# Experts' second product with tokens on the partitions, and an earlier pick of the first block

## The chip, the cores and the metric

One core of one Trainium2 chip. The metric is the device time of one execution in microseconds (us). All tensors are fp32.

## What is computed

```python
num = einsum('bhsm,bhmd->bhsd', phi(q), einsum('bhsm,bhsd->bhmd', phi(k), v))   # attention with random features
x = (num / den).reshape(2304, 512)
x = maximum(0.01 * (x @ w_in), x @ w_in) @ w_out           # dense, hidden width 2048
e = argmax(x @ w_gate, axis=1)                             # one of 8 experts for each token
gate = softmax(x @ w_gate)[e] * sigmoid(x @ w_output_gate)[e]
out[mask_e] = gate * (maximum(x[mask_e] @ w1[e], 0) @ w2[e])     # 512 -> 1024 -> 512, mask_e: tokens of expert e
```

With the inputs of the case the experts that have tokens get 576, 576 and 1152 of the 2304, and of the first 1792 tokens (chunks 0 to 6 below) 576, 576 and 640 are theirs.

## The kernel before

Every fp32 factor of the large products is split into two F32R parts, hi and lo (`hi_lo`, L208 on ScalarE for hi, L211 on VectorE for lo), and a product is three matmuls: hi·hi, lo·hi, hi·lo.

**Dense stage.** Tokens go in 9 chunks (0 to 8) of 256. For a chunk `c` and a step `u` of 8, `h_unit` makes 256 columns of the hidden layer (24 matmuls of 256 moving columns, L462 to L464), ScalarE copies them (L467), VectorE applies the leaky step (L468) and makes `gh` (L210) and `gl` (L211); `x_unit` adds their part of the output (12 matmuls of 512 columns, L481 to L483). The main loop writes `h_unit` of the next pair ahead of `x_unit` of this one, so TensorE runs H(8,1), X(8,0), H(8,2), X(8,1) and so on. When a chunk is done, `route_item` transposes its rows (L506), makes the gate's logits, picks an expert for each token, scatters the tokens' numbers into the table `tab_d` (L593, two indirect DMAs issued by GpSimd) and writes the rows to `x1_d` in DRAM (L597, SyncE's queue). Routing of chunk c runs beside chunk c+1, that of chunk 8 beside the first block of the experts.

**Experts.** A slot is 576 tokens of one expert, and a block is half a slot (288 tokens). Four slots are needed here. `Slot` reads the slot's part of the table into `idx` (L658) and loads 8 weight pieces of 512 KB (`weight(k)`, L664 and L666, on SyncE's queue) through two raw buffers (`wst`, tag `wraw`, 2 buffers) and converts each (hi L208 on ScalarE, lo L211 on VectorE). A block gathers its rows (`rows`, L681, 3 indirect DMAs of 96 rows), transposes them (`xt`, L692, 3 transposes for each of 4 pieces `d`), makes 8 pieces of the hidden layer (`hidden`, 12 matmuls of 288 columns each, L705 to L707; then ScalarE's relu L708 and VectorE's rest L709), and then the output with features on the partitions (`back`, for each of 4 `d` 24 matmuls of 288 columns, L718 to L720, copied by ScalarE, L721). `store` turns this into rows of tokens (4 transposes for each of 3 groups, L729), scales them (L731, L733) and scatters them to the output (L734).

The first slot is picked by `early()` among the experts whose first 576 tokens are known to be there, when chunk 7 has been routed, that is, while chunk 8 runs; its idx, its 8 weights (two for each of the last four steps of chunk 8) and the rows of its first block come then. All other slots come from `listed()`, after chunk 8's routing. A block's rows are gathered while the block before it runs (`following.rows()` at f == 3), its transposes stand between the `back(d)` of the block before. SyncE waits for the table (`behind`) before idx.

A scheduler writes the order on each engine, and an engine takes its instructions in that order. The order that matters is that of ScalarE and VectorE, which share weight conversion, the dense stage's `g`, and what the experts' products need.

Of the kernel before, what the change touches and what calls it, by code (L numbers as in the profile page):

```python
# [14 lines left out]
I32 = mybir.dt.int32  # L15
# [19 lines left out]
HALF = SLOT // 2  # L35
SUB = 96
NSUB = HALF // SUB
# [50 lines left out]
def tile_kernel(ctx: ExitStack, tc: tile.TileContext, kT, k_nat, v_nat, qT, q_nat, om, w_in, w_out, wg, w1, w2, out, stop=None, dbg=None):  # L88
# [46 lines left out]
    with ExitStack() as pa:  # L135
# [23 lines left out]
        def pads():  # L159
            padv = wst.tile([P, NE * NBLK * SLOT // P], I32, name="padv", tag="w32")  # L160
            nc.gpsimd.iota(padv, pattern=[[0, NE * NBLK * SLOT // P]], base=NTOK, channel_multiplier=0)
            nc.sync.dma_start(tab_d.rearrange("(p n) o -> p (n o)", p=P), padv)

            zero = wst.tile([P, 2, ROW], F32, name="zero", tag="wraw")
            nc.gpsimd.memset(zero, 0.0)
            nc.sync.dma_start(x1_d[NTOK - CH:NTOK, :].rearrange("(t p) n -> p t n", p=P), zero)
            nc.sync.dma_start(x1_d[NTOK:NTOK + 1, :], zero[0:1, 0, :])
# [332 lines left out]
        def route_item(c, rows):  # L500
            st = {}

            def tr(t):
                tv = ps_h.tile([P, D], F32, name="rtp", tag="h")
                for d in range(ND):
                    nc.tensor.transpose(tv[:, d * P:(d + 1) * P], rows[:, t, d * P:(d + 1) * P], ident)  # L506
                if t == 0:
                    if eb is None:
                        th = sb.tile([P, ND, CH], F32R, name="rth", tag="xh", bufs=3)
                        tl = sb.tile([P, ND, CH], F32R, name="rtl", tag="xl", bufs=3)  # L510
                    else:
                        th = eb.tile([P, ND, CH], F32R, name="rth", tag="eyr", bufs=1)
                        tl = eb.tile([P, ND, CH], F32R, name="rtl", tag="ey", bufs=1)
# [128 lines left out]
        tabv = tab_d.rearrange("(c p i) o -> c p (i o)", p=SUB, i=2 * NSUB)  # L642
# [5 lines left out]
        class Slot:  # L648


            def __init__(self, num, exp, at, first=False):
                self.c = nc.values_load(num[0:1, ds(at, 1)], engines=[SP], min_val=0, max_val=NC - 1)
                self.e = nc.values_load(exp[0:1, ds(at, 1)], engines=[SP], min_val=0, max_val=NE - 1)
                self.first = first
                self.w = []
                pool = rt if first else eb
                self.idx = pool.tile([SUB, 2 * NSUB], I32, name="idx", tag="idx", bufs=1 if first else 3)
                got = nc.sync.dma_start(self.idx, tabv[ds(self.c, 1)].rearrange("o p i -> (o p) i"))  # L658
                behind(got.ins, [o for k, o in placed if k == placed[-1][0]], "the table whole")
# [12 lines left out]
        class Block:  # L672
            def __init__(self, slot, half):
                self.slot = slot
                self.idx = slot.idx[:, half * NSUB:(half + 1) * NSUB]
                self.first = slot.first and half == 0

            def rows(self):
                self.xr = eo.tile([SUB, NSUB, ROW], F32, name="exr", tag="exr", bufs=2)
                for i in range(NSUB):  # L680
                    nc.gpsimd.indirect_dma_start(  # L681
                        out=self.xr[:, i, :], out_offset=None, in_=x1_d[:, :],
                        in_offset=bass.IndirectOffsetOnAxis(ap=self.idx[:, i:i + 1], axis=0))

            def xt(self, d):
                if d == 0:
                    pool, bufs = (eo, 1) if eb is None else (eb, 2)
                    self.xh = pool.tile([P, ND, HALF], F32R, name="exh", tag="exh", bufs=bufs)
                    self.xl = pool.tile([P, ND, HALF], F32R, name="exl", tag="exl", bufs=bufs)
                t = ps_proj.tile([P, 512], F32, name="ext", tag="pj")[:, 0:HALF]  # L690
                for i in range(NSUB):
                    nc.tensor.transpose(t[:, i * SUB:(i + 1) * SUB], self.xr[:, i, d * P:(d + 1) * P], ident[0:SUB, 0:SUB])  # L692
                hi_lo(self.xh[:, d, :], self.xl[:, d, :], t, nc.scalar, nc.vector)
                if d == ND - 1:
                    self.scale = eo.tile([SUB, NSUB], F32, name="esc", tag="esc", bufs=3)
                    nc.gpsimd.tensor_copy(self.scale, self.xr[:, :, D])

            def hidden(self, f):
                if f == 0:
                    self.hh = eb.tile([P, EFF // P, HALF], F32R, name="ehh", tag="ehh", bufs=1)  # L700
                    self.hl = eb.tile([P, EFF // P, HALF], F32R, name="ehl", tag="ehl", bufs=1)
                t = ps_a.tile([P, 512], F32, name="eht", tag="a")[:, 0:HALF]
                for d in range(ND):
                    wh, wl = (w[:, f * P:(f + 1) * P] for w in self.slot.w[d])
                    nc.tensor.matmul(t, wh, self.xh[:, d, :], start=d == 0, stop=False)  # L705
                    nc.tensor.matmul(t, wh, self.xl[:, d, :], start=False, stop=False)  # L706
                    nc.tensor.matmul(t, wl, self.xh[:, d, :], start=False, stop=d == ND - 1)  # L707
                nc.scalar.activation(self.hh[:, f, :], t, AF.Relu)  # L708
                nc.vector.scalar_tensor_tensor(self.hl[:, f, :], t, 0.0, f32(self.hh[:, f, :]), op0=ALU.max, op1=ALU.subtract)  # L709

            def back(self, d):
                if d == 0:
                    self.y = eb.tile([P, ND, HALF], F32, name="ey", tag="ey", bufs=1)
                t = ps_x.tile([P, 512], F32, name="eyt", tag="x")[:, 0:HALF]
                nf = EFF // P
                for f in range(nf):
                    wh, wl = (w[:, (f % 2) * D + d * P:(f % 2) * D + (d + 1) * P] for w in self.slot.w[4 + f // 2])
                    nc.tensor.matmul(t, wh, self.hh[:, f, :], start=f == 0, stop=False)  # L718
                    nc.tensor.matmul(t, wh, self.hl[:, f, :], start=False, stop=False)  # L719
                    nc.tensor.matmul(t, wl, self.hh[:, f, :], start=False, stop=f == nf - 1)  # L720
                nc.scalar.copy(self.y[:, d, :], t)  # L721

            def store(self, i, apart=True, final=False):
                if i == 0:
                    self.yr = eb.tile([SUB, NSUB, D], F32, name="eyr", tag="eyr", bufs=1)
                ps, tag = (ps_a, "a") if final and i == 2 else (ps_h, "h")
                t = ps.tile([P, 512], F32, name="eot", tag=tag)[0:SUB]
                for d in range(ND):
                    nc.tensor.transpose(t[:, d * P:(d + 1) * P], self.y[:, d, i * SUB:(i + 1) * SUB], ident)  # L729
                if i == 1:  # L730
                    nc.scalar.activation(self.yr[:, i, :], t, AF.Copy, scale=self.scale[:, i:i + 1])  # L731
                else:
                    nc.vector.tensor_scalar_mul(self.yr[:, i, :], t, self.scale[:, i:i + 1])  # L733
                ins = nc.gpsimd.indirect_dma_start(  # L734
                    out=out[:, :], out_offset=bass.IndirectOffsetOnAxis(ap=self.idx[:, i:i + 1], axis=0),
                    in_=self.yr[:, i, :], in_offset=None, bounds_check=NTOK - 1, oob_is_err=False)
# [64 lines left out]
        for i, (c, u) in enumerate(pairs):  # L801
# [28 lines left out]
            if c == NCH - 1 and not flow and not routes:  # L830
                if slot is None:
                    slot = early()
                    block = Block(slot, 0)
                    pq.close()
                    eo = ctx.enter_context(tc.tile_pool(name="eo", bufs=2, side="right", reuse_waits="tile"))
                    block.rows()
                for k in range(len(slot.w), 8 if u == NU - 1 else min(8, len(slot.w) + 2)):
                    slot.weight(k)
# [24 lines left out]
    with ExitStack() as pb:  # L863
        eb = pb.enter_context(tc.tile_pool(name="eb", bufs=2, reuse_waits="tile"))
        late = [f for it in routes for f in it if f is not nop]
        prev = None
        for s in range(NSLOT + 1):
            for half in range(2):
                last = s == NSLOT and half == 1
                for f in range(EFF // P):  # L870
                    block.hidden(f)
                    if prev is not None and 1 <= f <= NSUB:
                        prev.store(f - 1)
# [11 lines left out]
                for d in range(ND):  # L885
# [5 lines left out]
        for i in range(NSUB):  # L891
            prev.store(i, final=True)

        n_slots = nc.values_load(nsl[0:1, 0:1], min_val=NSLOT, max_val=NSLOT + NE)
        with tc.For_i(NSLOT, n_slots) as s:  # L895
# [3 lines left out]
            for half in range(2):  # L899
# [6 lines left out]
                for d in range(ND):  # L906
                    b_.back(d)
                for i in range(NSUB):
                    b_.store(i, False)
# [69 lines left out]
```

## Time and profile before

| | |
|---|---|
| median of 3 runs | 900.98 us (895.33 to 901.02) |
| the profiled execution | 894.16 us, span 892.4 us |
| TensorE busy | 834.9 us, 94% of the span |
| mean granted clock of TensorE | 0.983 |
| VectorE, ScalarE, GpSimd busy | 456.5, 316.7, 184.5 us |

The profile gives each instruction's start and duration on its engine; matmuls are pipelined, so a matmul's rate is read from the distance between two starts and not from its duration. A number in brackets behind an instruction is the time that the engine stood idle before it, with what ended that. Engines: PE is TensorE, PEld its weight load, ACT ScalarE, DVE VectorE, POOL GpSimd, SP SyncE (SPq: its DMA queue). [...]

### The profile page before, as it was taken

To read this page: it belongs to the slowest core of one execution; us is meant where nothing else is said; L and a number is where in the kernel's file an instruction comes from. 1 tells how busy PE (TensorE), PEld (TensorE's weight loads), DVE (VectorE), ACT (ScalarE), POOL (GpSimd) and SP (SyncE) were. 2 spreads that over 40 slices of the span, in tenths; PEclk is the share of its full clock that TensorE was granted. 3 is DMA by queue.
4 is the path that set the end of the run, shared out by engine and by line. 5 is a ranking of instruction groups with operands and counts; after the bars stand their busy time and mean duration, and the time that the engine had idled before them with its cause. 6 is when DMAs were issued, how large, how long until landed. Compare 5 with 4: busy or idle time off the path is not lost. (4 is left out here: it accounts for less than half of the span.)

```text
span 892.4 us, 14811 instructions
## 1 busy us (share of the span) xinstructions
PE 834.9 (94%) x5699; PEld 757.9 (85%) x5699; DVE 456.5 (51%) x1149; ACT 316.7 (35%) x783; POOL 184.5 (21%) x257
## 2 busy tenths in 40 slices
PE   9789898899899999999999999998759899999995
PEld 7678776799799899888889898987759899999994
DVE  6999789535445455545454444344625433522220
ACT  4766556333333223323332232112414423422221
POOL 3645535202121011121010000001033112311111
PEclk9999999999999999999999999999979999999998
DMA  7646655101442021242020000005156532500001
GB/s 228 206 134 191 195 160 164 59 4 58 64 98 66 8 41 48 54 89 66 1 48 1 24 1 2 24 25 168 48 150 193 166 100 77 172 26 29 28 28 29
DMA packets 45564, 73.07 MB, mean 82 GB/s; under 512 B 5681, under 2 KB 28337, under 8 KB 45490
## 3 DMA queue, kind: packets, MB, share of 16 engines
q1 hardware_dynamic: 41842, 62.61, 25.0%
q0 software_dynamic: 3648, 9.47, 3.8%
q8 instruction: 47, 0.77, 0.4%
q14 instruction: 27, 0.22, 0.1%
HBM read 62.00 MB, written 10.07 MB: 81 GB/s over the span
## 5 line engine op out<-in xcount | busy, mean ns | idle before, releaser
L462 PE MATMUL hp<-xh,wih 128*128 128x256 f32 x576 | 166.4, 289 | 2.7 <-DVE xl L211 2.1
L463 PE MATMUL hp<-xl,wih 128*128 128x256 f32 x576 | 161.9, 281 | 0.1
L464 PE MATMUL hp<-xh,wil 128*128 128x256 f32 x576 | 161.5, 280 | 0.0
L481 PE MATMUL acc<-woh,gh 128*128 128x512 f32 x288 | 123.1, 428 | 7.0 <-DVE gh L210 5.6
L318 ACT ACTIVATE h<-pw,bias 128x128 f32<-128x128 f32 x288 | 84.8, 373 | 105.1 <-DVE bias L310 85.4
L468 DVE SCALAR_TENSOR_TENSOR g<-hp,g 128x512 f32<-128x512 f32 x72 | 49.6, 688 | 133.3 <-ACT g L467 121.9
L483 PE MATMUL acc<-woh,gl 128*128 128x512 f32 x288 | 115.0, 400 | 0.2 <-DVE gl L211 0.2
L482 PE MATMUL acc<-wol,gh 128*128 128x512 f32 x288 | 114.1, 396 | 0.0
L462 PEld LDWEIGHTS hp<-xh,wih 128*128 128x128 f32 x576 | 108.8, 189 | 6.2 <-issue 2.5
L463 PEld LDWEIGHTS hp<-xl,wih 128*128 128x128 f32 x576 | 108.8, 189 | 2.2 <-DVE xl L211 0.3
L464 PEld LDWEIGHTS hp<-xh,wil 128*128 128x128 f32 x576 | 108.8, 189 | 0.0
L467 ACT COPY g<-hp 128x512 f32<-128x512 f32 x72 | 42.3, 587 | 131.9 <-PE hp L464 131.7
L705 PE MATMUL eht<-exh,ewh 128*128 128x288 f32 x256 | 80.0, 313 | 2.4 <-ACT exh L208 1.4
L706 PE MATMUL eht<-exl,ewh 128*128 128x288 f32 x256 | 77.2, 302 | 1.3 <-DVE exl L211 1.3
L718 PE MATMUL eyt<-ehh,ewh 128*128 128x288 f32 x256 | 78.2, 305 | 0.0
L719 PE MATMUL eyt<-ehl,ewh 128*128 128x288 f32 x256 | 76.8, 300 | 0.3 <-DVE ehl L709 0.3
L707 PE MATMUL eht<-exh,ewl 128*128 128x288 f32 x256 | 76.8, 300 | 0.0
L720 PE MATMUL eyt<-ehh,ewl 128*128 128x288 f32 x256 | 76.5, 299 | 0.0
L289 PE MATMUL pw<-om_raw,xpair 128*128 128x256 f32 (+1 forms) x260 | 70.3, 385 | 3.3 <-ACT h L318 3.3
L269 POOL TENSOR_TENSOR nat<-nat 128x256 f32<-128x256 f32 (+1 forms) x65 | 44.7, 690 | 139.0 <-DMA nat<-q_nat 65.8
L481 PEld LDWEIGHTS acc<-woh,gh 128*128 128x128 f32 x288 | 54.2, 188 | 18.8 <-DVE gh L210 6.5
L483 PEld LDWEIGHTS acc<-woh,gl 128*128 128x128 f32 x288 | 54.0, 188 | 14.3 <-DVE gl L211 2.4
(157 smaller groups left out, 1552.8 us busy)
## 6 DMA issues: line engine op xcount, KB each, us to landing
eraw<-w SPq DMA_DIRECT2D x32, 512.0 KB
wraw<-w_in SPq DMA_DIRECT2D x16, 512.0 KB
wraw<-w_out SPq DMA_DIRECT2D x16, 512.0 KB
x_d<-rows SPq DMA_DIRECT2D x9, 514.0 KB
xpair<-qT SPq DMA_DIRECT2D x18, 256.0 KB
nat<-q_nat SPq DMA_DIRECT2D x30, 128.0 KB
nat<-k_nat SPq DMA_DIRECT2D x27, 128.0 KB
xpair<-kT SPq DMA_DIRECT2D x12, 256.0 KB
```

Source lines behind the costliest of these rows:

```text
L318: nc.scalar.activation(h[:, j, :], src[:, j // 2, j % 2], AF.Exp, bias=bias[:, j:j + 1], scale=sc)
L462: nc.tensor.matmul(hp[:, i, :], a, xh[:, d, :], start=d == 0, stop=False)
L463: nc.tensor.matmul(hp[:, i, :], a, xl[:, d, :], start=False, stop=False)
L464: nc.tensor.matmul(hp[:, i, :], b_, xh[:, d, :], start=False, stop=d == ND - 1)
L481: nc.tensor.matmul(acc[t], a, h_, start=u == 0 and i == 0, stop=False)
L482: nc.tensor.matmul(acc[t], a, l_, start=False, stop=False)
L483: nc.tensor.matmul(acc[t], b_, h_, start=False, stop=u == NU - 1 and i == 1)
L705: nc.tensor.matmul(t, wh, self.xh[:, d, :], start=d == 0, stop=False)
L706: nc.tensor.matmul(t, wh, self.xl[:, d, :], start=False, stop=False)
L707: nc.tensor.matmul(t, wl, self.xh[:, d, :], start=False, stop=d == ND - 1)
L718: nc.tensor.matmul(t, wh, self.hh[:, f, :], start=f == 0, stop=False)
L719: nc.tensor.matmul(t, wh, self.hl[:, f, :], start=False, stop=False)
```

## The change

`back` works on a tile of up to 128 tokens: the hidden tile is stationary and 512 columns of the weight move, so the output has tokens on the partitions and is scaled and scattered straight away. `store`, its transposes and the copy `ey` are gone. A slot's 576 tokens are 5 tiles (four of 128 and one of 64), and the blocks are 256 and 320 tokens. The first slot is picked when chunk 6 has been routed (`early()` at c == NCH - 2); the rows of both its blocks are gathered at the start of chunk 8, and its 8 weights are loaded one for each step of chunk 8.

```diff
+PARTS = [[(0, P), (1, P)], [(2, P), (3, P), (4, SLOT - 4 * P)]]
...
             def rows(self):
-                self.xr = eo.tile([SUB, NSUB, ROW], F32, name="exr", tag="exr", bufs=2)
-                for i in range(NSUB):
+                self.xr = eo.tile([P, 3, ROW], F32, name="exr", tag="exr", bufs=2)
+                for j, (i, r) in enumerate(self.tiles):
                     nc.gpsimd.indirect_dma_start(
-                        out=self.xr[:, i, :], out_offset=None, in_=x1_d[:, :],
...
-            def back(self, d):
...
+            def back(self, j, apart=True, final=False):
+                i, r = self.tiles[j]
...
+                t = ps_x.tile([P, D], F32, name="eyt", tag="x")[0:r]
                 nf = EFF // P
                 for f in range(nf):
...
+                    wh, wl = (w[:, (f % 2) * D:(f % 2 + 1) * D] for w in self.slot.w[4 + f // 2])
+                    a, b_ = (h[:, f, j * P:j * P + r] for h in (self.hh, self.hl))
+                    nc.tensor.matmul(t, a, wh, start=f == 0, stop=False)
+                    nc.tensor.matmul(t, a, wl, start=False, stop=False)
+                    nc.tensor.matmul(t, b_, wh, start=False, stop=f == nf - 1)
+                scale = self.scale[0:r, j:j + 1]
+                if final and j == 2:
+                    nc.scalar.activation(yr[:, 0:D // 2], t[:, 0:D // 2], AF.Copy, scale=scale)
+                    nc.vector.tensor_scalar_mul(yr[:, D // 2:D], t[:, D // 2:D], scale)
+                elif j == 1:
+                    nc.vector.tensor_scalar_mul(yr, t, scale)
                 else:
...
+                    nc.scalar.activation(yr, t, AF.Copy, scale=scale)
...
+            if c == NCH - 1 and u == 0:
+
+                assert not flow and slot is not None
+                pq.close()
+                eo = ctx.enter_context(tc.tile_pool(name="eo", bufs=2, side="right", reuse_waits="tile"))
+                block, second = Block(slot, 0), Block(slot, 1)
+                block.rows()
+                second.rows()
...
-            if c == NCH - 1 and not flow and not routes:
-                if slot is None:
-                    slot = early()
...
-                for k in range(len(slot.w), 8 if u == NU - 1 else min(8, len(slot.w) + 2)):
-                    slot.weight(k)
+            if slot is None and c == NCH - 2 and not routes and not any(c_ < 0 for c_, _ in flow):
+                slot = early()
+            if c == NCH - 1:
+                slot.weight(u)
...
-                        following = Block(slot, 1) if half == 0 else Block(other, 0)
-                        following.rows()
-                for d in range(ND):
-                    block.back(d)
-                    if not last:
-                        following.xt(d)
-                prev, block = block, None if last else following
+                        following = second if s == half == 0 else Block(slot, 1) if half == 0 else Block(other, 0)
+                        if following is not second:
+                            following.rows()
+                for j in range(len(block.tiles)):
+                    if not last and j < 2:
+                        following.xt(2 * j)
+                        following.xt(2 * j + 1)
+                    block.back(j, final=last)
+                block = None if last else following
```

What is not shown: idx is read by two DMAs instead of one, `x1_d`'s rows of the chunks not yet routed are filled with zeros, and two small buffers change their tags.

On GpSimd, before, from the table's scatters of chunks 6 to 8 on (L593); `exr` are a block's gathered rows, `esc` its scales:

```order
L593 DMA tab_d<-tokid,r_pi 18432x1 x4
L681 DMA exr<-x_d,idx 96x514 x3
L696 COPY esc<-exr 96x3
L593 DMA tab_d<-tokid,r_pi 18432x1 x2
L681 DMA exr<-x_d,idx 96x514 x6
```

and now, from the scatters of chunk 6 on:

```order
L594 DMA tab_d<-tokid,r_pi 18432x1 x2
L685 DMA exr<-x_d,idx 128x514 x4
L685 DMA exr<-x_d,idx 64x514
L700 COPY esc<-exr 128x2 x2
L703 COPY esc<-exr 64x1
L594 DMA tab_d<-tokid,r_pi 18432x1 x4
```

The gathers of both blocks of the first slot now stand ahead of the table's scatters of chunks 7 and 8; before, the first block's stood behind those of chunk 7 and the second block's behind those of chunk 8.

On ScalarE in chunk 8, before; `ewh` is the hi part of a weight piece of the first slot, `g` the dense stage's copy:

```order
L208 CAST ewh<-eraw 128x1024 x2
L467 COPY g<-hp 128x512
L208 CAST ewh<-eraw 128x1024 x2
L467 COPY g<-hp 128x512
L208 CAST ewh<-eraw 128x1024 x2
L467 COPY g<-hp 128x512
L208 CAST ewh<-eraw 128x1024 x2
```

and now, from the first weight piece on:

```order
L209 CAST ewh<-eraw 128x1024
L468 COPY g<-hp 128x512
L860 COPY rows<-acc_6125 128x512
L209 CAST ewh<-eraw 128x1024
L468 COPY g<-hp 128x512
L209 CAST rth<-rtp 128x4x128
L209 CAST ewh<-eraw 128x1024
L209 CAST rth<-rtp 128x4x128
L209 CAST exh<-ext 128x256
L529 COPY side<-lgp 32x256
L209 CAST ewh<-eraw 128x1024
L468 COPY g<-hp 128x512
```

Weight pieces stood in pairs ahead of the copies `g` of the last steps; now they stand one by one, spread over the chunk.

On VectorE where the first slot's first block ends and its second begins, now; `exl` is the lo part of the second block's transposed rows, `ewl` that of the second slot's weights, `ehl` that of the hidden layer:

```order
L717 SCALAR_TENSOR_TENSOR ehl<-eht,ehh 128x256 x2
L212 TENSOR_TENSOR exl<-ext,exh 128x320 x2
L212 TENSOR_TENSOR ewl<-eraw,ewh 128x1024 x2
L212 TENSOR_TENSOR exl<-ext,exh 128x320 x2
L212 TENSOR_TENSOR ewl<-eraw,ewh 128x1024
L738 TENSOR_SCALAR eyr<-eyt,esc 128x512
L212 TENSOR_TENSOR ewl<-eraw,ewh 128x1024
L717 SCALAR_TENSOR_TENSOR ehl<-eht,ehh 128x320
L212 TENSOR_TENSOR ewl<-eraw,ewh 128x1024
L717 SCALAR_TENSOR_TENSOR ehl<-eht,ehh 128x320 x2
```

Two weight pieces of the second slot stand ahead of the last two pieces of the second block's rows, and four stand ahead of the rest of its first hidden piece; ScalarE's order is the same in kind.

## Rows read from the trace of the kernel before

**Rows 1.** The page's parts 1 and 2: busy time, and PE in 40 slices.

```profile
PE 834.9 (94%) x5699; PEld 757.9 (85%) x5699; DVE 456.5 (51%) x1149; ACT 316.7 (35%) x783; POOL 184.5 (21%) x257
...
PE   9789898899899999999999999998759899999995
```

**Rows 2.** Windows: stretch, busy time (x instructions) of each engine, PEclk granted clock, DMA.

```profile
584.94:634.19 49.25, 41.48 (x259) 34.90 (x257) 25.31 (x57) 14.30 (x23) 4.92 (x6) 0.99 0.35 109
...
710.00:720.00 10.00, 8.50 (x52) 8.20 (x53) 5.84 (x8) 4.86 (x10) 4.49 (x4) 0.83 0.58 161
```

**Rows 3.** Waits of PE from 610 us on: total us, times, longest.

```profile
PE ext L692 <- DMA exr<-x_d,idx: 10.0, 3, 6.6
PE acc L481 <- DVE gh L210: 5.6, 3, 2.6
```

**Rows 4.** Timeline of PE at the second block's transposes: start, duration, instruction, [idle before].

```profile
653.78 0.29 PE L720 MATMUL eyt<-ehh,ewl 128*128 128x288 f32 x1
660.66 0.42 PE L692 MATMUL ext<-ident,exr 96*128 96x96 f32 x1 [6.58 <-DMA exr<-x_d,idx]
...
664.95 0.42 PE L692 MATMUL ext<-ident,exr 96*128 96x96 f32 x1 [3.12 <-DMA exr<-x_d,idx]
...
665.71 0.44 PE L720 MATMUL eyt<-ehh,ewl 128*128 128x288 f32 x1
...
670.75 0.34 PE L720 MATMUL eyt<-ehh,ewl 128*128 128x288 f32 x1
```

**Rows 5.** Timeline of PE: matmuls of 512, then of 288 columns, a half-slot's period, the end.

```profile
622.49 0.39 PE L481 MATMUL acc<-woh,gh 128*128 128x512 f32 x1
...
624.36 0.40 PE L483 MATMUL acc<-woh,gl 128*128 128x512 f32 x1
...
876.00 0.29 PE L718 MATMUL eyt<-ehh,ewh 128*128 128x288 f32 x1
...
879.97 1.62 PE L729 MATMUL eot<-ident,ey 128*96 128x128 f32 x12
...
802.56 0.49 PE L729 MATMUL eot<-ident,ey 128*96 128x128 f32 x3
...
830.47 0.60 PE L729 MATMUL eot<-ident,ey 128*96 128x128 f32 x4
```

**Rows 6.** Timeline of PE in chunk 8: the stalls of its last steps.

```profile
627.82 0.50 PE L481 MATMUL acc<-woh,gh 128*128 128x512 f32 x1 [2.56 <-DVE gh L210]
...
633.26 1.22 PE L692 MATMUL ext<-ident,exr 96*128 96x96 f32 x6 [2.12 <-DVE exl L211]
634.19 0.59 PE L705 MATMUL eht<-exh,ewh 128*128 128x288 f32 x1
```

**Rows 7.** Timelines of ACT and DVE: weight pieces converted.

```profile
622.01 1.05 ACT L208 CAST ewh<-eraw 128x1024 fp32r<-128x1024 f32 x1 [2.47 <-DMA eraw<-w]
...
628.19 1.05 ACT L208 CAST ewh<-eraw 128x1024 fp32r<-128x1024 f32 x1 [2.27 <-DMA eraw<-w]
...
662.70 1.04 ACT L208 CAST ewh<-eraw 128x1024 fp32r<-128x1024 f32 x1 [11.35 <-DMA eraw<-w]
...
625.47 1.22 DVE L211 TENSOR_TENSOR ewl<-eraw,ewh 128x1024 fp32r<-128x1024 f32 x1 [1.16 <-ACT ewh L208]
```

**Rows 8.** Timelines of POOL and of SP's queue: scatters, gathers, first weight of slot 1.

```profile
560.38 0.97 POOL L593 DMA_INDIRECT tab_d<-tokid,r_pi  x1 [0.30 <-issue]
...
607.55 0.96 POOL L681 DMA_INDIRECT exr<-x_d,idx  x1 [9.93 <-DMA idx<-tab_d]
...
613.65 0.18 POOL L696 COPY esc<-exr 96x3 f32<-96x3 f32 x1 [2.69 <-DMA exr<-x_d,idx]
...
648.11 0.96 POOL L593 DMA_INDIRECT tab_d<-tokid,r_pi  x1 [0.31 <-issue]
...
884.50 0.92 POOL L734 DMA_INDIRECT out_dram<-eyr,idx  x1 [0.30 <-issue]
...
656.60 11.77 SPq L664 DMA_DIRECT2D eraw<-w  x4
```

More of the change, by code (lines that the diff above doesn't have):

```diff
@@ L34 @@
 SLOT = 576
-HALF = SLOT // 2
-SUB = 96
-NSUB = HALF // SUB
+PARTS = [[(0, P), (1, P)], [(2, P), (3, P), (4, SLOT - 4 * P)]]
+PART = SLOT - 2 * P
 NBLK = NTOK // SLOT
@@ L165, in pads @@
             nc.gpsimd.memset(zero, 0.0)
-            nc.sync.dma_start(x1_d[NTOK - CH:NTOK, :].rearrange("(t p) n -> p t n", p=P), zero)
+            for c in (NCH - 2, NCH - 1):
+                nc.sync.dma_start(x1_d[c * CH:(c + 1) * CH, :].rearrange("(t p) n -> p t n", p=P), zero)
             nc.sync.dma_start(x1_d[NTOK:NTOK + 1, :], zero[0:1, 0, :])
@@ L511, in tr @@
                     else:
-                        th = eb.tile([P, ND, CH], F32R, name="rth", tag="eyr", bufs=1)
-                        tl = eb.tile([P, ND, CH], F32R, name="rtl", tag="ey", bufs=1)
+                        th = eb.tile([P, ND, CH], F32R, name="rth", tag="eyr", bufs=2)
+                        tl = eb.tile([P, ND, CH], F32R, name="rtl", tag="eyr", bufs=2)
                     st["t"] = (th, tl)
@@ L656, in __init__ @@
                 pool = rt if first else eb
-                self.idx = pool.tile([SUB, 2 * NSUB], I32, name="idx", tag="idx", bufs=1 if first else 3)
-                got = nc.sync.dma_start(self.idx, tabv[ds(self.c, 1)].rearrange("o p i -> (o p) i"))
-                behind(got.ins, [o for k, o in placed if k == placed[-1][0]], "the table whole")
+                self.idx = pool.tile([P, 5], I32, name="idx", tag="idx", bufs=1 if first else 3)
+                whole = tabv[ds(self.c, 1), 0:4 * P].rearrange("o (p i) -> (o p) i", i=4)
+                rest = tabv[ds(self.c, 1), 4 * P:SLOT].rearrange("o (p i) -> (o p) i", i=1)
+                for dst, src in ((self.idx[:, 0:4], whole), (self.idx[0:SLOT - 4 * P, 4:5], rest)):
+                    got = nc.sync.dma_start(dst, src)
+                    behind(got.ins, [o for k, o in placed if k == placed[-1][0]], "the table whole")
             def weight(self, k):
@@ L674, in __init__ @@
                 self.slot = slot
-                self.idx = slot.idx[:, half * NSUB:(half + 1) * NSUB]
-                self.first = slot.first and half == 0
+                self.tiles = PARTS[half]
+                self.n = sum(r for _, r in self.tiles)
             def rows(self):
-                self.xr = eo.tile([SUB, NSUB, ROW], F32, name="exr", tag="exr", bufs=2)
-                for i in range(NSUB):
+                self.xr = eo.tile([P, 3, ROW], F32, name="exr", tag="exr", bufs=2)
+                for j, (i, r) in enumerate(self.tiles):
                     nc.gpsimd.indirect_dma_start(
-                        out=self.xr[:, i, :], out_offset=None, in_=x1_d[:, :],
-                        in_offset=bass.IndirectOffsetOnAxis(ap=self.idx[:, i:i + 1], axis=0))
+                        out=self.xr[0:r, j, :], out_offset=None, in_=x1_d[:, :],
+                        in_offset=bass.IndirectOffsetOnAxis(ap=self.slot.idx[0:r, i:i + 1], axis=0))
             def xt(self, d):
@@ L687, in xt @@
                     pool, bufs = (eo, 1) if eb is None else (eb, 2)
[L688 to L692, printed above, removed]
@@ L693, in xt @@
-                hi_lo(self.xh[:, d, :], self.xl[:, d, :], t, nc.scalar, nc.vector)
-                if d == ND - 1:
-                    self.scale = eo.tile([SUB, NSUB], F32, name="esc", tag="esc", bufs=3)
-                    nc.gpsimd.tensor_copy(self.scale, self.xr[:, :, D])
+                    self.xh = pool.tile([P, ND, PART], F32R, name="exh", tag="exh", bufs=bufs)
+                    self.xl = pool.tile([P, ND, PART], F32R, name="exl", tag="exl", bufs=bufs)
+                t = ps_proj.tile([P, 512], F32, name="ext", tag="pj")[:, 0:self.n]
@@ new lines, in xt @@
+                for j, (_, r) in enumerate(self.tiles):
+                    nc.tensor.transpose(t[:, j * P:j * P + r], self.xr[0:r, j, d * P:(d + 1) * P], ident[0:r, 0:r])
+                hi_lo(self.xh[:, d, 0:self.n], self.xl[:, d, 0:self.n], t, nc.scalar, nc.vector)
+                if d == ND - 1:
+                    self.scale = eo.tile([P, 3], F32, name="esc", tag="esc", bufs=3)
+                    nc.gpsimd.tensor_copy(self.scale[:, 0:2], self.xr[:, 0:2, D])
+                    if len(self.tiles) == 3:
+                        r = self.tiles[2][1]
+                        nc.gpsimd.tensor_copy(self.scale[0:r, 2:3], self.xr[0:r, 2, D:D + 1])
@@ L698, in hidden @@
             def hidden(self, f):
                 if f == 0:
-                    self.hh = eb.tile([P, EFF // P, HALF], F32R, name="ehh", tag="ehh", bufs=1)
-                    self.hl = eb.tile([P, EFF // P, HALF], F32R, name="ehl", tag="ehl", bufs=1)
-                t = ps_a.tile([P, 512], F32, name="eht", tag="a")[:, 0:HALF]
+                    self.hh = eb.tile([P, EFF // P, PART], F32R, name="ehh", tag="ehh", bufs=1)
+                    self.hl = eb.tile([P, EFF // P, PART], F32R, name="ehl", tag="ehl", bufs=1)
@@ L703, in hidden @@
+                n = self.n
+                t = ps_a.tile([P, 512], F32, name="eht", tag="a")[:, 0:n]
                 for d in range(ND):
                     wh, wl = (w[:, f * P:(f + 1) * P] for w in self.slot.w[d])
[L705 to L708, printed above, removed]
@@ L709, in hidden @@
-                nc.vector.scalar_tensor_tensor(self.hl[:, f, :], t, 0.0, f32(self.hh[:, f, :]), op0=ALU.max, op1=ALU.subtract)
-            def back(self, d):
-                if d == 0:
-                    self.y = eb.tile([P, ND, HALF], F32, name="ey", tag="ey", bufs=1)
-                t = ps_x.tile([P, 512], F32, name="eyt", tag="x")[:, 0:HALF]
+                    nc.tensor.matmul(t, wh, self.xh[:, d, 0:n], start=d == 0, stop=False)
+                    nc.tensor.matmul(t, wh, self.xl[:, d, 0:n], start=False, stop=False)
@@ new lines, in hidden @@
+                    nc.tensor.matmul(t, wl, self.xh[:, d, 0:n], start=False, stop=d == ND - 1)
+                nc.scalar.activation(self.hh[:, f, 0:n], t, AF.Relu)
+                nc.vector.scalar_tensor_tensor(self.hl[:, f, 0:n], t, 0.0, f32(self.hh[:, f, 0:n]), op0=ALU.max, op1=ALU.subtract)
+            def back(self, j, apart=True, final=False):
+                i, r = self.tiles[j]
+                if j % 2 == 0:
+                    self.yr = eb.tile([P, 2, D], F32, name="eyr", tag="eyr", bufs=2)
+                yr = self.yr[0:r, j % 2, :]
+                t = ps_x.tile([P, D], F32, name="eyt", tag="x")[0:r]
@@ L715, in back @@
                 nf = EFF // P
                 for f in range(nf):
[L717 to L721, printed above, removed]
@@ L732, in store @@
                 else:
-                    nc.vector.tensor_scalar_mul(self.yr[:, i, :], t, self.scale[:, i:i + 1])
+                    nc.scalar.activation(yr, t, AF.Copy, scale=scale)
                 ins = nc.gpsimd.indirect_dma_start(
-                    out=out[:, :], out_offset=bass.IndirectOffsetOnAxis(ap=self.idx[:, i:i + 1], axis=0),
-                    in_=self.yr[:, i, :], in_offset=None, bounds_check=NTOK - 1, oob_is_err=False)
+                    out=out[:, :], out_offset=bass.IndirectOffsetOnAxis(ap=self.slot.idx[0:r, i:i + 1], axis=0),
@@ L738, in store @@
+                    in_=yr, in_offset=None, bounds_check=NTOK - 1, oob_is_err=False)
                 if apart:
@@ L871, in tile_kernel @@
                     block.hidden(f)
-                    if prev is not None and 1 <= f <= NSUB:
-                        prev.store(f - 1)
                     if late:
@@ L905, in tile_kernel @@
                     b_.hidden(f)
[L906 to L909, printed above, removed]
+                for j in range(len(b_.tiles)):
+                    b_.back(j, False)
 _NAMES = ["kT", "k_nat", "v_nat", "qT", "q_nat", "om", "w_in", "w_out", "wg", "w1", "w2"]
```

18 lines of the change are left out of this document (1 added, 17 removed).

## The prediction

> **What bounds the kernel now.** I read the busy shares first: TensorE works 94% of the span, and in its 40 slices only slices 31 and 32 (counted from 1; each is 22.3 us, so about 670 to 715 us) fall below 8 tenths [rows 1]. So the time is TensorE's work plus what it waits, and a change can gain by fewer or faster matmuls, by removing waits, or by a shorter end. I read the waits of TensorE next: from the last dense chunk on there are two large ones, 10.0 us for gathered rows `exr`, 5.6 us for `gh` in chunk 8 [rows 3]. Then the timeline around each. After the first block of the first slot, TensorE stands 6.58 and 3.12 us (and 0.3 between) for the second block's rows [rows 4], because these are gathered only after chunk 8's rows have been written and its table scattered. [...] In chunk 8 the window of 49.25 us has 41.48 busy [rows 2], so 7.8 idle: 5.6 for `gh` [rows 3], 2.12 for `exl` [rows 6]. These are weight conversions in pairs, ahead of `g` on ScalarE and VectorE. The last place is the end: the last product's matmul starts before 879.97 and the span ends at 892.4.
>
> **The second product, part by part.** Before, a half slot takes 27.91 us in the steady part (802.56 to 830.47) [rows 5]: 192 matmuls of 288 columns at 0.1323 are 25.4, and the remaining 2.5 us are its 24 transposes, 0.104 each. After, a whole slot has 192 hidden matmuls with the same columns in sum (256 and 320 instead of twice 288; the cost per column is what I assume constant) = 25.4, 120 matmuls of 512 columns, and 20 transposes for the rows. A 512-column matmul takes 0.234 us (8 steps from 622.49 to 624.36) [rows 5], so 28.1 us, and the transposes 2.1. Sum 55.6 for a slot against 55.8: -0.2, with four slots -0.9. So 24 x 8 matmuls become 24 x 5, each 1.77 times as long, and what the change saves are the 24 transposes (2.5 us a slot), which the partly filled fifth tile gives back: 64 tokens cost as much as 128. Both ends: -4 if a transpose of `store` costs 0.135 as at the end (1.62 us for 12) [rows 5], so 0.7 more saved a slot; +2 if the row transposes, now of 128 rows instead of 96, cost a third more (0.7 a slot). I take -1. ScalarE's copy `ey`, VectorE's and ScalarE's halves of the scaling are hidden in both versions.
>
> [...]
>
> **The end.** Before, 12 transposes (1.6 us), scaling, three scatters of 0.92 us one behind the other, and from the last scatter's end at 885.42 to the span's end 7.0 us [rows 5, 8]: 12.4 us from the last product. After, the last tile's scaling (halved between two engines) and one scatter remain: 0.3 + 0.45 + 0.2 + 0.92 + 7.0 = 8.9. -3.4; between -2.5 (the halved scaling is no faster) and -4.
>
> **The gathers.** All rows of the first slot now come after chunk 6's table. That scatter ends at 561.35; a gather started 9.93 us after the scatter's end before it [rows 8], so at 571.3; five gathers, 1.24 apart, and 2.7 to land [rows 8] end at 580 to 581. The second block's are wanted 70 us later; its stall of 10.0 us and the 2.6 of the low clock go: -12.6. The first block's are wanted at about 585 (its first transposes now stand near the start of chunk 8), 7 us behind the first tiles' landing; if they were late by more than that, all TensorE would wait. 576 rows is what the table surely has: an expert is full after chunk 6 here, so the pick is a real slot and no fifth slot appears.
>
> **Chunk 8.** One weight piece for each step, 1.05 us on ScalarE and 1.22 on VectorE [rows 7], instead of two. The copy `g` of a step can still stand behind one. From the order I count four places where TensorE still waits for such a step (second and third `g`, the `exh` of the first hidden piece, the one-hot of the routing), 1 us each: 4 instead of 7.8: -3.8; between 0 and -7.8.
>
> **The wait that comes.** The second slot's weights can't come sooner than chunk 8's routing, since the list of slots depends on it. Before, that scatter ends at 649.07, 14.9 us after the first hidden matmul (634.19), the first weight is issued 7.5 us later (656.60) and converted 6.1 us later still (662.70) [rows 6, 7, 8]. With the shorter first block (hidden pieces of 256 columns, the first one partly done in chunk 8, 2.4 us less) I put the first conversion at 26 us after the first block's start, t = 26. TensorE is done with the first block at 25.5 (10.4 hidden, 2.6 routing, 11.2 back, 1.2 transposes). On VectorE two weight pieces now stand ahead of the last rows `exl` of the second block and two more ahead of the `ehl` that frees the first hidden piece's buffer. Two raw buffers give 6.2 us for a pair (622.01 to 628.19) [rows 7]. So: `exl` is ready at t + 4 = 30 (4.5 us idle); two hidden pieces run to 33.5; `ehl` comes behind the second pair, at t + 6.2 + 3.9 = 36.1 (2.6 idle); the next `ehl` behind the third pair's first piece, 41.2, when TensorE is free at 37.9 (3.3 idle); 0.6 more at smaller places. 11.0 us in sum. After each idle of several us I add the low clock as it was seen (24 matmuls, 2.6 us) [rows 4] once: +13.6. Before, the same order stood there, but TensorE came 11 us later, held by its rows, so the weights did not show. Low end +2 (weights land much sooner than I count), high end +25 (below). Behind the waiting conversions on VectorE and ScalarE are `exl`, `ehl` and the relu, and TensorE waits for these.
>
> [...] If an engine could pass a waiting conversion, this wait would be near zero: the first rival.
>
> What was lost at the second slot's start (710 to 720: 1.5 us idle, clock 0.83, 1.4 us) [rows 2] has the same cause, weights behind; their queue now starts earlier against the block that needs them: -2.9, or 0.
>
> **Sum.** -12.6 - 3.8 - 1 - 3.4 - 2.9 + 13.6 = -10.1. The profiled execution took 894.16 us, so 884.1. The median of the runs is 900.98, and the runs spread from 895.33 to 901.02; the profiled one stands below them all, and I predict at its level, 884, knowing that at the median's level the same change would read 891. What the measurement can tell from no change is about 1%, 9 us.
>
> **The rivals.**
> A. The gathers' gain is not eaten: the weights come early enough or the order lets `exl` pass. Everything but the +13.6 stays: -23.7, 870; with chunk 8's stalls gone wholly 866. For it: ScalarE waited 11.35 us for that first weight [rows 7] with other traffic, the gathers, on the DMA queues, and that traffic is gone. Against: the 7.5 us from scatter to issue and the pair's 6.2 do not depend on it. 0.22.
> B. The forecast: the weights take the gather's place. 878 to 892. 0.55.
> C. Chunk 8 keeps its stalls, as seven single conversions each stand ahead of some `g` or `rth`, and the new wait is there: 888 to 894, within 1%. 0.13.
> D. Slower. The clock stays at the lower level through the whole second block, because it keeps waiting for weights: 96 hidden matmuls of 320 columns and 72 of 512 are 14.1 + 16.8 = 31 us; at the ratio seen (0.24 to 0.1323, so 0.81 more) +25 instead of +2.6, in sum +12: 906. It turns slower than before from 13 us of such work at the lower level (10.1/0.81), and slower by over 1% from 24. For it: the clock was at the lower level for 5 us after the one stall, and 0.83 in the stretch 710 to 720 after idles of only 2 us [rows 2, 4]. Against: with pieces of matmuls between, it came back within 24 matmuls. 0.05. The same sign has the first block's rows landing late in chunk 8: each us after 585 costs one, over 1% from 19 us late; 0.03.
> E. [...] 0.02.
>
> **The numbers.** 884 is B's. The range 866 to 897 takes in A at the low side, C and the smaller half of D at the high side, and leaves out E, the large half of D and A's far end, under 2 in 10. B alone is 878 to 892. Faster by over 1% against the runs before (below 892 at their median's level, a gain of 9 us): A, E and three quarters of B: 0.65. Within 1%: the rest of B, C and the small D: 0.28. Slower: 0.07.
>
> **What the profile after would show.** The 512-column matmuls of the second product 0.234 us apart; no wait for `exr` at the second block's transposes; instead idles before the second block's hidden matmuls, ended by VectorE's `exl` and `ehl`, with `ewl` just ahead of them, about 11 us in sum; `ewh` waiting for `eraw`, pairs 6.2 us apart; the granted clock near 0.5 for a few us after; chunk 8's idle about 4; from the last matmul to the end 9 us. Wrong would be: no idle there (A), idle in chunk 8 as before (C), a clock that stays down (D), or a wait for `exr` near 585.

## The result, and the profile after

The changed kernel takes 886.6 us (median of 7, 886.42 to 890.87) against 899.29 of the kernel before on the same chip; the ratio is 0.989, with a 95% interval from 0.9866 to 0.9914. The two medians as they stand are 12.7 us apart; the ratio, which counts here, makes it 9.9 us, and the prediction's sum said 10.1. The profiled execution has a span of 886.2 us, 6.2 less than that of before: the one profiled before happened to be among the quick ones, the one after among the longer ones.

The page of the changed kernel, busy time and the slices of PE and of the granted clock, which answer to [rows 1]:

```profile
PE 840.5 (95%) x5299; PEld 734.0 (83%) x5299; DVE 449.8 (51%) x1142; ACT 307.0 (35%) x755; POOL 179.5 (20%) x253
...
PE   9889998999999999999999999997996999999996
```

Besides the last slice, which is the end, two are low: 28 (598 to 620 us, chunk 8) and 31 (665 to 687 us, the second block). In [rows 1] they are 29 and 30, 624 to 669 us, and slice 2 and the last are low as well; the prediction counted them wrong, as 31 and 32 and as the only ones, which no number of it rests on. The waits of PE from 560 us on, which answer to [rows 3]:

```profile
PE eht L713 <- DVE ehl L717: 7.2, 3, 5.6
PE acc L484 <- DVE gl L212: 6.8, 2, 6.2
PE eht L713 <- ACT exh L209: 1.5, 2, 0.9
PE eyt L730 <- ACT ehh L716: 0.6, 1, 0.6
PE eht L714 <- DVE exl L212: 0.4, 1, 0.4
```

No wait for `exr` is left. In its place stand one of 5.6 us in the first slot's second block, as forecast, and one of 6.2 us in chunk 8, which was not. The timeline of PE at both, and at the last matmul, and POOL's last scatter:

```profile
618.66 0.80 PE L484 MATMUL acc<-woh,gl 128*128 128x512 f32 x1 [6.22 <-DVE gl L212]
619.25 0.63 PE L482 MATMUL acc<-woh,gh 128*128 128x512 f32 x1
...
622.67 0.63 PE L484 MATMUL acc<-woh,gl 128*128 128x512 f32 x1
...
666.57 0.41 PE L713 MATMUL eht<-exh,ewh 128*128 128x320 f32 x1 [0.87 <-ACT exh L209]
667.33 0.41 PE L714 MATMUL eht<-exl,ewh 128*128 128x320 f32 x1 [0.35 <-DVE exl L212]
...
675.72 0.64 PE L713 MATMUL eht<-exh,ewh 128*128 128x320 f32 x1 [5.63 <-DVE ehl L717]
...
877.65 0.40 PE L732 MATMUL eyt<-ewh,ehl 128*64 128x512 f32 x1
...
879.46 0.92 POOL L741 DMA_INDIRECT out_dram<-eyr,idx  x1 [4.91 <-DVE eyr L736]
```

After the 6.22 us the matmuls of 512 columns start 0.43 us apart (8 steps from 619.25 to 622.67) instead of 0.234: the granted clock is 0.50 of full speed from 618.70 to 622.70, as before from 665.71 to 670.75, behind the stalls of [rows 4].

I cut both profiled executions at the same places of the program. Each number is a difference of two starts in the timeline of PE or ACT; for the end of the last product after the change I add 0.23 us to the start of its last matmul, and the last row runs to the span's end.

| stretch | before | after | difference | predicted |
|---|---|---|---|---|
| up to chunk 7's rows (L850, L860) | 578.02 | 579.54 | +1.5 | 0 |
| chunk 8, to the first hidden matmul behind the last dense one | 56.17 | 58.29 | +2.1 | -3.8 |
| first slot (634.19 to 707.95; 637.83 to 705.78) | 73.76 | 67.95 | -5.8 | about +1 |
| three more slots, to the end of the last product (879.97; 877.88) | 172.02 | 172.10 | +0.1 | -3.6 |
| from there to the end | 12.43 | 8.32 | -4.1 | -3.4 |

The first row is mostly spread between executions: in the eight later profiles, of both kinds of kernel, that copy starts between 576.0 and 578.7. Eight hidden matmuls of the first slot (0.9 us) now run within chunk 8, so about 1 us of the second row belongs to the third.

### The profile page after: what moved, and what is told of

It reads as the page before. It is cut to its first block, busy times and chain, and to the rows that moved or that the text cites. A ratio compares the mean times of both kernels' runs of the same rounds, so it can differ in the third digit from the quotient of the medians.

```text
span 886.2 us, 13999 instructions
## 1 busy us (share of the span) xinstructions
PE 840.5 (95%) x5299; PEld 734.0 (83%) x5299; DVE 449.8 (51%) x1142; ACT 307.0 (35%) x755; POOL 179.5 (20%) x253
## 5 line engine op out<-in xcount | busy, mean ns | idle before, releaser
L713 PE MATMUL eht<-exh,ewh 128*128 128x256 f32 (+1 forms) x256 | 76.9, 301 | 8.9 <-DVE ehl L717 7.2
L714 PE MATMUL eht<-exl,ewh 128*128 128x256 f32 (+1 forms) x256 | 76.4, 298 | 0.4 <-DVE exl L212 0.4
L715 PE MATMUL eht<-exh,ewl 128*128 128x256 f32 (+1 forms) x256 | 76.0, 297 | 0.0
L212 DVE TENSOR_TENSOR ewl<-eraw,ewh 128x1024 fp32r<-128x1024 f32 x32 | 39.1, 1225 | 59.9 <-ACT ewh L209 49.8
L730 PE MATMUL eyt<-ewh,ehh 128*128 128x512 f32 (+1 forms) x160 | 64.3, 402 | 0.6 <-ACT ehh L716 0.6
L731 PE MATMUL eyt<-ewl,ehh 128*128 128x512 f32 (+1 forms) x160 | 63.4, 396 | 0.0
```

Of the source, the lines that this page charges most:

```text
L713: nc.tensor.matmul(t, wh, self.xh[:, d, 0:n], start=d == 0, stop=False)
L714: nc.tensor.matmul(t, wh, self.xl[:, d, 0:n], start=False, stop=False)
L715: nc.tensor.matmul(t, wl, self.xh[:, d, 0:n], start=False, stop=d == ND - 1)
L730: nc.tensor.matmul(t, a, wh, start=f == 0, stop=False)
```

## The experiments

**Each half alone.** `pick_only` is the kernel before with the four places of the early pick; `product_only` is the changed kernel with those places put back.

```diff
# pick_only, against the kernel before
...
+            if c == NCH - 1 and u == 0:
...
+                block, second = Block(slot, 0), Block(slot, 1)
+                block.rows()
+                second.rows()
...
+            if slot is None and c == NCH - 2 and not routes and not any(c_ < 0 for c_, _ in flow):
+                slot = early()
+            if c == NCH - 1:
+                slot.weight(u)
...
```

> The kernel before with the early pick alone (first slot picked when chunk 6 is routed, rows of both its blocks gathered at the start of chunk 8, one weight piece a step); its second product and blocks of 288 are kept. Theory (the pick gives the gain, the product nothing but the shorter end): no wait for exr at the second block, instead a wait for exl and ehl behind weight conversions as in the changed kernel, a long wait for gl in chunk 8 of about 6 us as there, the steady half slot at 27.9 us, the end at 12.4 us; about 7 us faster than before, ratio 0.992. Rival (the product gives the gain): ratio 0.998 or above.

> The changed second product and blocks of 256 and 320 alone; the first slot is picked after chunk 7 and its rows gathered as before. Theory: a slot in the steady part takes 56.7 us instead of 55.8 (row transposes cost more), four slots +3, the end 8.3 us instead of 12.4, the wait for exr at the second block stays at about 10 us; about 1 us faster than before, ratio 0.999. Rival (the product gives the gain): 6 us faster, 0.993.

`pick_only`: 0.9955 (0.9929 to 0.998), 4.0 us. `product_only`: 0.9943 (0.9915 to 0.9971), 5.1 us. Each half brings about half, and together they make the 9.9 (0.9955 x 0.9943 = 0.990). My theory before these runs, that the product gives nothing but its end, fell: I had set 56.7 us for an undisturbed slot after against the best slot before, 55.8, but slots before are not all undisturbed. From the first hidden matmul to slot 1's, `product_only` takes 71.6 us against 73.8, and to the end it saves 4.1. The waits of PE in `pick_only`, then in `product_only`:

```profile
PE eyt L719 <- ACT ey L722: 5.9, 1, 5.9
PE acc L482 <- DVE gh L211: 3.9, 1, 3.9
```

```profile
PE ext L696 <- DMA exr<-x_d,idx: 7.1, 2, 5.0
PE acc L482 <- DVE gh L211: 4.7, 4, 2.3
```

So it is the early pick that removes the wait for `exr` and brings a new one to each of the two places, though not by the same instructions. At the second block, in `pick_only` ScalarE's copy `ey` stands behind the weight pieces, where in the changed kernel `ehl` does on VectorE. In chunk 8 I had expected a wait of 6 us for `gl` behind the late piece, as in the changed kernel; in `pick_only` the piece was in time, so the 3.9 us for `gh` are not its work (below, where the late piece is told).

**The second block's wait: order, or weights too late?** In `w1_behind` the conversions of the second slot's pieces are ordered behind what the second block needs. Their loads stay where they were: the first is issued 10.9 us behind the write of chunk 8's rows, in the changed kernel 11.6.

```diff
             def weight(self, k, after=None):
...
+                with ExitStack() as order_:
+                    for i_ in after or ():
+                        order_.enter_context(tc.issue_after(i_.ins))
+                    hi_lo(hi, lo, raw, nc.scalar, nc.vector)
...
-                    if f >= 4 and s < NSLOT:
+                    if f >= 4 and 0 < s < NSLOT:
...
+                    if s == 0 and half == 1 and f in (2, 5):
+                        other.weight(len(other.w), block.h_done)
+                        other.weight(len(other.w), block.h_done)
...
+                    if s == 0 and half == 0 and j == 1:
+                        other.weight(0, following.x_done)
+                        other.weight(1, following.x_done)
+                    if s == 0 and half == 1 and j == 0:
+                        other.weight(6, block.h_done)
+                        other.weight(7, block.h_done)
```

> The changed kernel, with the conversions of the second slot's weight pieces ordered behind what the first slot's second block needs: pieces 0 and 1 behind its last rows, 2 and 3 behind its third hidden piece, 4 and 5 behind the sixth, 6 and 7 behind the eighth. Theory (the wait of the second block is one of order on ScalarE and VectorE): the idles ended by exl and ehl there go (6.9 us, and 1.7 of low clock), 7 us faster than the changed kernel, ratio to before 0.981. Rival (the pieces are only late, so they bind at the second slot's first hidden piece instead): ratio 0.989.

0.9837 (0.9775 to 0.9898), so about 5 us less than the changed kernel, where 7 were expected; the interval overlaps that of the changed kernel (0.9866 to 0.9914), and the reading rests on the rows. Windows of the stretch 650 to 690 (busy time of each engine, then PEclk), changed kernel and `w1_behind`:

```profile
650.00:690.00 40.00, 33.02 (x178) 28.48 (x177) 16.89 (x25) 15.33 (x25) 9.86 (x11) 0.96 0.54 169
```

```profile
650.00:690.00 40.00, 40.00 (x213) 34.14 (x212) 17.56 (x25) 15.43 (x26) 11.79 (x13) 1.00 0.61 190
```

The 7 us idle and the low clock are gone with the same weights. It was order. At the second slot's start TensorE waits 1.87 and 0.89 us for `ehl`, 2.8 in sum, against 2.2 in the changed kernel; so at most 0.6 us comes back, where the rival said all of it.

**Chunk 8's wait.** VectorE in the changed kernel, ahead of the 6.22 us:

```profile
608.51 0.43 DVE L211 CAST gh<-g 128x512 fp32r<-128x512 f32 x1
616.78 1.23 DVE L212 TENSOR_TENSOR ewl<-eraw,ewh 128x1024 fp32r<-128x1024 f32 x1 [7.84 <-ACT ewh L209]
617.92 0.68 DVE L212 TENSOR_TENSOR gl<-g,gh 128x512 fp32r<-128x512 f32 x1
```

VectorE stands 7.84 us before the first slot's last weight piece, and `gl` is behind it. In `w7_behind` that one conversion goes behind the last `g` of the chunk.

```diff
...
-                slot.weight(u)
+                slot.weight(u, g_done[0] if u == NU - 1 else None)
...
```

`g_done` holds the copy `g` and the `gl` of the step written last; `weight` takes its second argument as in `w1_behind`.

> The changed kernel, with the conversion of the first slot's last weight piece ordered behind the last g of chunk 8 on ScalarE and VectorE. Theory (in the changed kernel VectorE stands before gl of step 5 for that late piece; the 6.2 us idle and about 2.5 us of low clock after it are its whole price): no long wait for gl in chunk 8, 8 us faster than the changed kernel, ratio to before 0.980. Rival (the gain is given back at the next wait, the second slot's weights): ratio 0.988.

0.9824 (0.9762 to 0.9887), so about 6 us less than the changed kernel, where 8 were expected; here too the intervals overlap. Windows 600 to 640, changed kernel, then `w7_behind`:

```profile
600.00:640.00 40.00, 33.78 (x208) 29.92 (x208) 15.02 (x29) 8.01 (x13) 2.01 (x2) 0.91 0.28 33
```

```profile
600.00:640.00 40.00, 40.00 (x277) 35.94 (x275) 21.45 (x61) 11.34 (x24) 2.31 (x3) 1.00 0.26 35
```

The stall is gone, and the low clock behind it. The gain is not given back: chunk 8 to the rows of the last chunk takes 48.75 us (576.43 to 625.18) against 57.83 in the changed kernel.

**Both.**

> The changed kernel with both orders of conversions at once (the last weight piece of the first slot behind the last g of chunk 8, the second slot's pieces behind the second block's needs). Theory (two separate stalls): the two gains add, about 6 and 5 us less than the changed kernel each as measured one by one, so 12 to 15 us, ratio to before 0.974. Rival (both free the same time, and the second slot's weights then bind): 0.981.

869.62 us, ratio 0.9757 (0.9732 to 0.9782): the best of all kernels here, 14 us under the changed one (883.67, measured beside it; 13 by the ratios, 0.9904 less 0.9757), and here the intervals lie far apart. The two gains add: about 5 and 6 one by one, 13 together.

**Why the piece comes late.** It is issued at 604.40 and converted at 615.70, 11.3 us later. `after_again` is the changed kernel once more:

> The changed kernel once more, on the same chip as the other runs of this call. Theory: ratio to before 0.989, the last weight piece of the first slot lands 10 to 11 us after its issue again, and the long wait for gl in chunk 8 is there again at 5 to 6 us. Rival (that landing was an accident of one execution): it lands within 4 us, and no wait for gl over 2 us.

0.9904 (0.987 to 0.9938), issue 603.49, conversion 613.71, wait for `gl` 5.15 us: no accident. SP's queue, POOL and ACT in the changed kernel:

```profile
601.73 0.37 SPq L598 DMA_DIRECT2D x_d<-rows  x1
604.40 0.38 SPq L670 DMA_DIRECT2D eraw<-w  x1
...
602.64 0.98 POOL L594 DMA_INDIRECT tab_d<-tokid,r_pi  x1 [0.30 <-issue]
...
615.70 1.05 ACT L209 CAST ewh<-eraw 128x1024 fp32r<-128x1024 f32 x1 [7.95 <-DMA eraw<-w]
```

Two DMAs are under way when it is issued: the write of chunk 7's rows, ahead of it on the same queue (issued 2.7 us earlier; it takes 3.4 us to land in `w7_behind` and 3.6 in `w1_behind`), and the table's scatter of chunk 7, from GpSimd (issued 3.1 and 1.8 us earlier; 8.5 and 8.8 us to land there). Each was left out once, so that the tokens of chunk 7 get zero rows or no result.

> The changed kernel without the write of chunk 7's rows to x1_d (left out, so those tokens get zero rows). Theory S (the table's scatter, still under way when the last weight piece is issued, is what holds its DMA): the piece still takes about 10 us to land, the wait for gl stays near 6 us. Theory W (the write of the rows just ahead of it on the same queue holds it): it lands in about 4 us, and the wait for gl is under 1 us, some 8 us off the time.

> The changed kernel without the table's scatter of chunk 7 (left out, so those tokens get no result). Theory S (the scatter holds the last weight piece's DMA): it lands in about 4 us, the wait for gl is under 1 us, some 8 us off the time. Theory W (the write of the rows holds it): it still takes about 10 us to land, the wait for gl stays near 6 us.

Without the write (issue 601.15) the piece was as late; without the scatter (issue 602.04) it landed in 3.6 us. ACT in `no_write7`, then in `no_scatter7`:

```profile
612.18 1.04 ACT L209 CAST ewh<-eraw 128x1024 fp32r<-128x1024 f32 x1 [7.69 <-DMA eraw<-w]
```

```profile
605.59 1.06 ACT L209 CAST ewh<-eraw 128x1024 fp32r<-128x1024 f32 x1 [0.20 <-DMA eraw<-w]
```

The waits for `gl` were 6.0 and 0.6 us, the times 882.64 and 878.85 (one execution each, so this rests on the rows, not on the times). The scatter holds it: theory S. In `w7_behind` the piece lands as late, 10.1 us behind its issue, and nothing waits for it.

What is held depends on when it is issued. In `pick_only` the last piece is issued at 600.31, between the starts of the scatter's two DMAs (599.40 and 601.49), and the write of the rows behind it, at 600.93; with the time from issue to landing at the end:

```profile
x_d<-rows SPq DMA_DIRECT2D x1, 514.0 KB, 12.5
eraw<-w SPq DMA_DIRECT2D x1, 512.0 KB, 4.1
```

The piece lands in 4.1 us, and it is the write that takes 12.5, where it takes 3.4 and 3.6 ahead of the piece in `w7_behind` and `w1_behind`. It lands at 613.4, and TensorE, which waits 3.9 us for VectorE's `gh` in `pick_only`, goes on at 613.96; that `gh` waited for this write is not shown.

## Why the prediction was right, point by point

The sum came out near the measured change (-10.1 against -9.9 by the ratio; -12.7 by the medians, -6.2 between the two profiles that the table compares), and that it came so near is luck. Against the table, chunk 8 was 5.9 us worse than forecast, the first slot 6.8 better, the three later slots 3.7 worse. The mechanism, the gathers' wait gone and the weights' wait in its place, was right; the term of chunk 8 was not.

- **Gathers, -12.6: right.** The wait of 10.0 us [rows 3, 4] and the low clock behind it are gone. The 2.6 us of that clock, which the sum takes off here and adds once for the new wait, come from what was measured before: the 24 matmuls of 288 columns behind the stall start 0.24 us apart (21 steps from 665.71 to 670.75 [rows 4], granted clock 0.50), those at the end 0.1323 (30 steps from 876.00 to 879.97 [rows 5], granted clock 1.00), 24 x 0.108. The first block's rows never made TensorE wait, although they were gathered at 575.1 to 580.8, 4 us later than I worked out (the scatter ended 1.5 us later, and from its end to the first gather it took 12.2 us with two idx DMAs instead of 9.93).
- **The wait that comes, +13.6: right in kind, too dear.** The first conversion came 25.5 us behind the first block's start (663.30 less 637.83; I had 26). VectorE:

```profile
664.38 2.49 DVE L212 TENSOR_TENSOR ewl<-eraw,ewh 128x1024 fp32r<-128x1024 f32 x2 [11.15 <-ACT ewh L209]
666.79 0.88 DVE L212 TENSOR_TENSOR exl<-ext,exh 128x320 fp32r<-128x320 f32 x2
670.27 1.23 DVE L212 TENSOR_TENSOR ewl<-eraw,ewh 128x1024 fp32r<-128x1024 f32 x1 [2.60 <-issue]
...
674.04 1.22 DVE L212 TENSOR_TENSOR ewl<-eraw,ewh 128x1024 fp32r<-128x1024 f32 x1 [1.88 <-ACT ewh L209]
675.18 0.48 DVE L717 SCALAR_TENSOR_TENSOR ehl<-eht,ehh 128x320 fp32r<-128x320 f32 x1
```

`exl` behind two pieces, the first `ehl` behind two more: the chain as told. But the first wait was 1.2 us (0.87 + 0.35) and not 4.5, since `exl` was done at 667.7, 29.8 us behind the start, as worked out, while TensorE was done with the first block only at 664.65, 26.8 behind (I had 25.5) and was fed until 665.5 by what of the hidden piece needed only the first two row pieces. The second was 5.63 (I had 2.6), the third, 3.3 in my sum, did not show: its `ehl` was done at 679.07, 41.2 behind the start, as worked out, but TensorE, held longer by the second wait and then slower by the clock, had other work until 679.83, 42.0 behind the start (I had 37.9). In `after_again` the second wait is 4.18 and the third does show, with 1.56. So 6.9 us idle, and about 1.2 us for the ten matmuls of 320 columns at the lower clock (granted 0.50 from 675.60 to 678.60; 0.268 apart instead of 0.147), 8 instead of 13.6. The first slot got 5.8 us shorter.
- **Chunk 8, -3.8: wrong, +2.1** (about +1 without the hidden matmuls that moved there). I counted how many conversions stand ahead of a `g`, and took each for at most its own duration, 1.05 or 1.22 us. Two of my four places showed (0.65 and 0.62 us). What I did not do is ask when the data of each piece is there: I priced the queue, not the DMA behind it. The last piece was 11 us under way because chunk 7's scatter was. The rows that I had read of before could not show it: there no weight is loaded beside a scatter, since idx waits for the scatter and the weights for idx [rows 8]. But its trace does show it, in the attention stage, where GpSimd waits for loads `nat` from SyncE's queue. The end of a scatter, a load 1.3 us behind it, its use, the next load and its use:

```profile
381.56 0.96 POOL L593 DMA_INDIRECT tab_d<-tokid,r_pi  x1 [0.31 <-issue]
383.78 0.33 SPq L258 DMA_DIRECT2D nat<-q_nat  x1
391.26 0.51 POOL L269 TENSOR_TENSOR nat<-nat 128x192 f32<-128x192 f32 x1 [7.89 <-DMA nat<-q_nat]
393.39 0.33 SPq L258 DMA_DIRECT2D nat<-q_nat  x1
395.62 0.61 POOL L269 TENSOR_TENSOR nat<-nat 128x256 f32<-128x256 f32 x1 [2.64 <-DMA nat<-q_nat]
```

The first load takes 7.5 us from issue to use, the second, larger one 2.2. Of the loads `nat` that GpSimd waited for there, the three issued 0.8 to 2.7 us behind a table scatter's issue took 7.4 to 10.6 us, two issued about 8 us behind it 6.8 and 7.5, and the 21 issued over 10 us behind it 2.1 to 3.3. A piece held for 7 us would have been a bound for this term. Mine were 0 and -7.8, and the term fell outside.
- **The product, -1.** The matmuls of 512 columns do start 0.233 apart, those of the tile of 64 tokens as those of 128. An undisturbed slot takes 56.72 us (765.31 to 822.03), 0.9 more than 55.8, and not 0.2 less; the step that failed is the row transposes. I had 2.1 us for 20; the six of a 320-token block's pair of pieces take 1.08 us (651.08 to 652.16), so twice that, and the four of a 256-token block 0.36, so 2.9 in all. Whether the 64-row transposes themselves cost that or the changes between 128 and 64 rows was not tried.
- **The second slot's start, -2.9: mostly wrong.** 2.2 us idle are still there; only the low clock (1.4) is gone (granted clock 1.00 from 710 to 720 instead of 0.83). Over three slots -3.6 was forecast for this and the product, +0.1 came.
- **The end, -3.4: right,** -4.1: from the last matmul's end at 877.88 to the last scatter's end at 880.38, then 5.8 us where I had taken 7.0 [rows 8]; why it is shorter stays open.
- **The rivals.** A (no new wait) is false for the changed kernel, but `w1_behind` shows that it takes only another order. C named the place in chunk 8 (7.5 us idle there, as much as before), yet by many small conversions; most of it was one, by its DMA. D's clock came back within 6 us both times: the granted clock is 1.00 again from 624.13 on, 5.5 us behind the first matmul after the one stall (618.66), and from 678.77 on, 3.1 us behind that after the other (675.72). E, at 0.02, has none of the runs for it: matmuls of 512 columns start 0.233 us apart in a stream in every one of them.

## What to carry to other kernels

When work is moved earlier, look at what else is on the DMA queues at its new place, and not only at what stands around it on the engines: here a load issued 0.8 us behind a scatter took 10.1 to 11.3 us, and 3.6 without the scatter, and a case of that stood in the trace of before, in another stage (7.5 us against 2.2). Look then at the conversions that wait for a DMA in the order of an engine that also feeds TensorE: here VectorE stood 7.84 us before such a one, and TensorE 6.22 us for the `gl` behind it. Put it behind what TensorE needs next, if its result is wanted much later (here worth 13 us at two places, more than the change itself). A sum that comes out right is no proof of its terms: cut both profiles at the same places and compare each stretch.

## What the runs showed of the hardware

A 512 KB load issued 0.8 us after the end of a scatter's issue (two indirect DMAs of 128 single 4-byte elements) took 10.1 to 11.3 us to land in five profiles, against 3.6 us without that scatter. That it is the scatter and not the 514 KB write ahead on the load's own queue was shown by leaving out each, in one execution each (11.0 us without the write, 3.6 without the scatter). A load issued between the starts of the scatter's two DMAs landed in 4.1 us, and a write 0.6 us behind that load took 12.5 instead of 3.4 to 3.6. How the scatter holds the others was not tried.
